# A state-space layer and a gated FFN in one kernel: decays computed early, the first pair left unnormalised, two input loads moved

## The chip, the cores and the metric

The kernel runs on one core of a Trainium2 chip. The metric is the device time of one execution in microseconds. Engines are named as the profile names them: PE (TensorE), DVE (VectorE), ACT (ScalarE), POOL (GpSimd) and SP (SyncE, which here only issues DMAs). L12 is line 12 of the kernel before.

## The reference

Inputs are x (4, 8, 768, 32), a (4, 8, 768), B and C (4, 8, 768, 16), all float32: batch, heads, sequence, and head or state size. The first half is a linear recurrence with a decay per step, written in chunks; the second half is a gated FFN over all 3072 tokens (256 to 1536 to 256).

```python
log_a = np.log(np.clip(a, 1e-06, 1.0))
for c in range(nc):                                   # chunks of 32
    cum = np.cumsum(la, axis=-1)
    L = np.exp(cum[..., :, None] - cum[..., None, :]) * causal
    M = np.einsum('bhin,bhjn->bhij', Cc, Bc) * L
    y_intra = np.einsum('bhij,bhjd->bhid', M, xc)
    y_inter = np.einsum('bhin,bhnd->bhid', Cc, state) * np.exp(cum)[..., None]
    y[:, :, sl] = y_intra + y_inter
    state = decay_full * state + sum_j Bx             # Bx: B outer x, decayed to the chunk's end
...
x = y.transpose(0, 2, 1, 3).reshape(B * S, H * D)
out = (np.maximum(x @ w_gate, 0.0) * (x @ w_val)) @ w_out
```

The kernel uses longer chunks than the reference (128 positions, in pairs of 256) and bfloat16 matmuls.

## The kernel before

**Tiling.** The 3072 tokens are 12 pairs of 256 positions, three pairs to a batch; a pair holds two chunks. The FFN runs over 6 blocks of 512 tokens, two pairs each. Before the loop over blocks, pairs 0 and 1 are done by straight code; in block b the FFN of block b runs while the recurrence of later pairs is worked in between. The order of instructions on each engine is the order of the program text: `in_order` chains them, and there is no planner.

**Decays.** A running product of a over each window of 256 positions is a scan on DVE (`product`, L215). `a_first` holds the first window of two batches (16 rows), `a_sb` all 96 windows. Each position's decay has to lie on the partition of that position, so the products are turned by float32 matmuls: `dec_wide` (L232, four matmuls) for the pairs below `NWIDE` = 4, whose positions lie two to a partition, and `dec_all` (L242, two matmuls) for all. `wfac` and `fac` hold, for B, one over the decay, and for C, the decay. The right operand normalises by the decay at the window's end: `pfirst` (the identity times one over the last product, L221 and L222) for pair 0 and the first window of batch 1, `pick` (L190, L827) for the rest.

**One pair.** `scale_bc` (L334) multiplies B and C by their factors into bf16; `transp` and `bevac`, `cevac` (L378 to L415) turn them to BT and CT; `G` (L444) multiplies them into four PSUM banks, `gevac` (L458) masks these on ACT (with POOL's causal selection) and DVE; `back` turns BT back; `astep` (L500) accumulates the state matmuls in `A_ps`; `sevac` (L517) copies the state to `Sd`; `Dm` and `inter` (L623, L599) make y, and `yevac` (L637) writes yT. Between windows of one batch the state is multiplied by `over`, the decay over a window, per partition (head). `over` is made by `dec_end` (L255), which broadcasts the last products to all partitions, and by `over_sum` and `over_sum2` (L260, L269) on DVE, which keep of each partition its own head.

**FFN.** `gvh_mm`, `gvh_relu`, `gvh_mul` (L744 to L765) do half a block (256 tokens) for one f of 12, `gv` (L731) a whole one (512); gate and val lie in the five shared PSUM banks (tag "shared"). `fout` (L775) multiplies by w_out.

**Queues.** SP issues a, and then most loads of B, C and x, in order; ACT issues three early loads; POOL issues the weights. `held` (L850) loads a pair behind a small memset on DVE, so that the issue waits until DVE reaches it. `keep_warm` (L198) issues matmuls of ones whose result is not used.

**The early order.** Pair 0: scan of `a_first`, `dw` (L819, its decays), scaling (L822, L823), transposes, G, back; then `d12` (L881, decays of pairs 1 and 2), the state step, Dm, inter, yevac; pair 1 the same way, with the first FFN matmuls in between. `dall` and the end decays are made at L930 to L935, copied by ACT at L953 to L957.

Of the kernel before, what the change touches and what calls it, by code (L numbers as in the profile page):

```python
# [8 lines left out]
FP32 = mybir.dt.float32  # L9
# [20 lines left out]
def kernel(  # L30
# [84 lines left out]
    even = const.tile([128, 24], FP32)  # L115
# [11 lines left out]
    load_bc(0, 1, nc.sync)  # L127
    new_x(0)
    load_x(0, 1, nc.scalar)
# [74 lines left out]
    keep_warm(6)  # L204
    keep_warm(1, 384)
# [3 lines left out]
    cp_first = glob.tile([2 * NH, 256], FP32)  # L209
    rfirst = const.tile([2 * NH, 1], FP32)  # L210
    pfirst = const.tile([2 * NH, 2 * NH], FP32)
# [8 lines left out]
    product(cp_first, a_first, 2 * NH)  # L220
    nc.vector.reciprocal(rfirst, cp_first[:, 255:256])  # L221
    nc.vector.tensor_scalar_mul(pfirst, identf[0:2 * NH, 0:2 * NH], rfirst)  # L222
    product(cp, a_sb, W3 * BH)
# [18 lines left out]
    def dec_all(d):  # L242
        for i in range(2):
            nc.tensor.matmul(
                out=d[:, i].rearrange("p w b h -> p (w b h)"),
                lhsT=cp[:, i * 128:(i + 1) * 128],
                rhs=pick.rearrange("p w h -> p (w h)"),
                start=(i == 0), stop=True, skip_group_check=True)


    ends = const.tile([W3 * BH, 128], FP32)
    over = const.tile([128, NB], FP32)
    over2 = const.tile([128, NB], FP32)

    def dec_end(d):  # L255

        nc.tensor.matmul(out=d, lhsT=ends, rhs=pick[:, 1], start=False, stop=True,
                         skip_group_check=True)

    def over_sum(de):  # L260
        own = smask.rearrange("p t (q d) -> p (t q) d", q=4)[:, :, 0]
        prod = const.tile([128, NB, 8], FP32)
        nc.vector.tensor_tensor(
            out=prod, in0=de.rearrange("p (b h) -> p b h", b=NB),
            in1=own.rearrange("p (o h) -> p o h", o=1).to_broadcast([128, NB, 8]),
            op=ALU.mult)
        nc.vector.tensor_reduce(out=over, in_=prod, op=ALU.add, axis=mybir.AxisListType.X)

    def over_sum2(de):  # L269
        own = smask.rearrange("p t (q d) -> p q t d", q=4)[:, :, :, 0]  # L270
# [608 lines left out]
    for i in range(2):  # L879
        load_x(2, i, nc.sync)  # L880
# [275 lines left out]
```

## Time and profile before

| | |
|---|---|
| time, median of 3 runs | 123.42 us (122.86 to 124.12) |
| the profiled execution's own time | 123.24 us |
| its span in the profile | 121.5 us, 3331 instructions |
| busy: PE, DVE, ACT, POOL | 97%, 74%, 61%, 43% |
| DMA traffic | 13.69 MB, mean 113 GB/s |

The span is the profiled part of the execution, from the first instruction to the last; the time holds 1.7 us more. A line of the timeline gives start, length, engine, line, operation, written tile, read tiles, shapes, and how many equal instructions were merged; in brackets the engine's idle time before it and what ended it. A float32 matmul shows as two passes. Matmul ends are modelled, so spacing from start to start says more than length.

### The profile page before, as it was taken

The numbers are of one execution on the slowest core, as the hardware profiler recorded it, in microseconds if no ns is written. First come the engines' busy times: TensorE is split into PE (matmuls) and PEld (weight loads), VectorE is DVE, ScalarE is ACT, GpSimd is POOL, SyncE is SP. The second block draws the span as 40 slices with busy tenths as digits, with TensorE's granted clock in tenths as the row PEclk, the third lists the DMA queues.
The fourth block names the chain that finished last, engine by engine and source line by source line (L and its number), as shares of the span: only waits on it lengthen the run. The fifth ranks groups of instructions, "written<-read, shape, count | busy, mean of one in ns | idle before, by whom it ended". The sixth has DMA issues, their size and how long they took to land.

```text
span 121.5 us, 3331 instructions
## 1 busy us (share of the span) xinstructions
PE 117.3 (97%) x1238; PEld 75.3 (62%) x1238; DVE 89.6 (74%) x214; ACT 73.8 (61%) x160; POOL 52.1 (43%) x105
## 2 busy tenths in 40 slices
PE   7999999999999999999999999999999999999990
PEld 2446854676786477888477644578544677444790
DVE  5978878986999956899876588765778766578500
ACT  4177886840898734888744767625767445776340
POOL 6879999842615073768058252633400033000000
PEclk9999999999999999999999999999999999999999
DMA  3999999959997999799996799941300002200022
GB/s 59 212 195 172 191 197 206 187 86 126 165 105 157 98 125 154 91 131 218 117 148 139 73 127 113 291 94 58 115 0 5 0 0 92 86 0 0 0 86 86
DMA packets 80591, 13.69 MB, mean 113 GB/s; under 512 B 73424, under 2 KB 80576, under 8 KB 80576
## 3 DMA queue, kind: packets, MB, share of 16 engines
q1 hardware_dynamic: 73088, 10.54, 55.4%
q0 software_dynamic: 4080, 2.36, 13.8%
q10 hardware_dynamic: 3408, 0.59, 2.6%
q8 instruction: 9, 0.15, 0.6%
q14 instruction: 6, 0.05, 0.1%
HBM read 11.12 MB, written 3.15 MB: 117 GB/s over the span
## 4 chain that ended last, share of the span: by engine, by line
PE 93%; DVE 4%; issue 0%; DVEq 0%
PE o L783 25%; PE val L738 19%; PE gate L738 19%; PE gv L753 13%; PE w L200 4%; PE g L452 2%; PE g L491 2%; PE y L678 1%; PE y L630 1%; PE o L795 1%; PE tp L389 1%; DVE gs L475 1%; DVE CT L415 1%; DVE Sm L546 1%; PE y L619 1%; DVE bs L344 1%
## 5 line engine op out<-in xcount | busy, mean ns | idle before, releaser
L742 DVE TENSOR_TENSOR h<-r,val 128x512 bf16<-128x512 bf16 x54 | 36.9, 687 | 9.3 <-ACT r L741 6.4
L741 ACT ACTIVATE r<-gate 128x512 bf16<-128x512 f32 x54 | 32.3, 597 | 12.1 <-PE gate L738 11.3
L783 PE MATMUL o<-wo,h 128*128 128x256 bf16 x276 | 33.5, 273 | 0.0
L738 PE MATMUL val<-yT,wv 128*128 128x512 bf16 x108 | 32.6, 379 | 0.0
L738 PE MATMUL gate<-yT,wg 128*128 128x512 bf16 x108 | 32.6, 379 | 0.0
L783 PEld LDWEIGHTS <-h 128*128 128x128 bf16 x276 | 25.8, 98 | 5.4 <-issue 1.2
L171 POOL TENSOR_SCALAR_AFFINE_SELECT gs<-gs 128x512 bf16<-128x512 bf16 (+1 forms) x24 | 12.2, 533 | 22.1 <-ACT gs L464 22.1
L475 DVE TENSOR_TENSOR gs<-g,masks 128x512 bf16<-128x512 f32 x24 | 15.4, 685 | 6.0 <-PE g L491 2.8
L738 PEld LDWEIGHTS <-wv 128*128 128x128 bf16 x108 | 10.4, 98 | 12.8 <-DMA wv<-in_moe_w_val_dram 0.8
L738 PEld LDWEIGHTS <-wg 128*128 128x128 bf16 x108 | 10.4, 98 | 11.1
L464 ACT CAST gs<-g 128x512 bf16<-128x512 f32 x12 | 7.0, 587 | 15.7 <-PE g L452 7.3
L763 DVE TENSOR_TENSOR h<-r,gv 128x256 bf16<-128x256 bf16 x36 | 13.9, 417 | 0.9 <-ACT r L760 0.7
L760 ACT ACTIVATE r<-gv 128x256 bf16<-128x256 f32 x36 | 13.6, 388 | 1.2
L753 PE MATMUL gv<-yT,wg 128*128 128x256 bf16 x72 | 13.9, 273 | 0.0
L753 PE MATMUL gv<-yT,wv 128*128 128x256 bf16 x72 | 13.8, 273 | 0.0
L297 POOL TENSOR_TENSOR bz<-bcr,fac 128x512 bf16<-128x512 f32 x6 | 6.4, 1060 | 11.7 <-DMA bcr<-in_B_dram 9.4
L811 ACT COPY ob<-o 128x512 f32<-128x512 f32 x11 | 6.5, 592 | 4.1 <-PE o L783 4.0
L318 ACT CAST yT<-y 128x512 bf16<-128x512 f32 (+1 forms) x9 | 4.6, 528 | 5.4 <-PE y L678 3.4
L318 POOL CAST xb<-xr 128x512 bf16<-128x512 f32 (+1 forms) x10 | 6.0, 597 | 4.2 <-DMA xr<-in_x_dram 3.1
L753 PEld LDWEIGHTS <-wv 128*128 128x128 bf16 x72 | 7.0, 98 | 0.8
L753 PEld LDWEIGHTS <-wg 128*128 128x128 bf16 x72 | 6.7, 98 | 1.1 <-issue 0.2
L200 PE MATMUL w<-const-bfloat16-1.0 128*128 128x512 bf16 (+3 forms) x16 | 6.2, 511 | 0.8 <-PEq L1140 0.8
(119 smaller groups left out, 110.5 us busy)
## 6 DMA issues: line engine op xcount, KB each, us to landing
xr<-in_x_dram SPq DMA_DIRECT2D x23, 128.0 KB, 3.3
out_dram<-ob SPq DMA_DIRECT2D x9, 256.0 KB, 2.7
bcr<-in_B_dram SPq DMA_DIRECT2D x16, 64.0 KB, 3.0
bcr<-in_C_dram SPq DMA_DIRECT2D x16, 64.0 KB, 3.0
wg<-in_moe_w_gate_dram POOLq DMA_DIRECT2D x6, 128.0 KB, 5.5
wv<-in_moe_w_val_dram POOLq DMA_DIRECT2D x6, 128.0 KB, 5.4
wo<-in_moe_w_out_dram POOLq DMA_DIRECT2D x3, 256.0 KB, 6.9
out_dram<-ob SPq DMA_DIRECT2D x4, 128.0 KB, 2.2
```

The lines of the kernel that those rows point to most:

```text
L171: nc.gpsimd.affine_select(out=dst, in_=dst, pattern=pattern, compare_op=ALU.is_ge, fill=0.0, base=0, channel_multiplier=-1)
L200: nc.tensor.matmul(out=w[:, 0:cols], lhsT=nc.const_aps.tensor(1.0, [128, 128], BF16), rhs=nc.const_aps.tensor(1.0, [128, cols], BF16), sta ...
L318: (eng.copy if eng is nc.scalar else eng.tensor_copy)(out=out, in_=in_)
L464: nc.scalar.copy(out=d[:, 0], in_=g[0])
L475: nc.vector.tensor_tensor(out=d[:, q], in0=g[q], in1=m, op=ALU.mult)
L738: nc.tensor.matmul(out=o, lhsT=w_tile(ws, f, k), rhs=yT[:, k, tk], start=(k == 0), stop=(k == 1), skip_group_check=True)
L741: nc.scalar.activation(r, g, AF.Relu)
L742: nc.vector.tensor_tensor(out=fst[b][:, f], in0=r, in1=v, op=ALU.mult)
L753: nc.tensor.matmul(out=gv_[:, j], lhsT=w_tile((wgs, wvs)[j], f, k), rhs=yT[:, k, tk], start=(k == 0 and not (early and j)), stop=(k == 1), ...
L760: nc.scalar.activation(r[:, 0:256], fst[b, f, u][:, 0], AF.Relu)
L763: nc.vector.tensor_tensor(out=fst[b][:, f, u * 256:(u + 1) * 256], in0=fst.pop((b, f, u, "r"))[:, 0:256], in1=fst.pop((b, f, u))[:, 1], op ...
L783: nc.tensor.matmul(out=o[:, ts % 2], lhsT=fst[b][:, f, ts * 128:(ts + 1) * 128], rhs=wo[:, f], start=(f == 0 and new), stop=(f == NF - 1), ...
```

## The change

It does five things.

- **Pair 0 is not normalised.** `a_first` is 8 rows instead of 16; `rfirst` and `pfirst` go, and `dw` multiplies by the identity. The state after pair 0 is therefore scaled by the window's decay when it is read: `sevac` multiplies by a fifth column of `over` and keeps a float32 copy, `before[0]`; the next state steps start anew and add `before[0]`, or `before[1]`, which is `before[0]` times `over` of batch 0, made on POOL.
- **The scan of all of a** stands behind the scaling of pair 0, `rmid` and `pick` behind CT.
- **Loads.** C of pair 0 goes second on ACT's queue, x of pair 0's second chunk to SP; its cast goes from DVE to ACT. x of pair 2 is loaded behind h of f = 8 of block 0 (before: ahead of `d12`), and so x of pair 3 stands behind it; the cast of pair 2 moves into the first third of `fout`, that of pair 3 from POOL to ACT.
- **All decays early.** `dec_wide` for pairs 1 and 2, and for pair 3, `dec_all` and a new `dec_middle` fill one PSUM tile, `decays`, in the place of `d12` and two fillers. `dec_middle` makes `over` by five one-column matmuls against `head_of`, which five ACT copies fill at the start. `dec_end`, `over_sum`, `over_sum2` go.
- **Filler.** `keep_warm` calls are shortened or dropped.

```diff
-    a_first = glob.tile([2 * NH, 256], FP32)
-    nc.sync.dma_start(out=a_first, in_=a[0:2, :, 0:256].rearrange("b h s -> (b h) s"))
+    a_first = glob.tile([NH, 256], FP32)
+    nc.sync.dma_start(out=a_first, in_=a[0, :, 0:256])
...
     load_bc(0, 0, nc.scalar)
-    load_bc(0, 1, nc.sync)
+    load_bc(0, 1, nc.scalar)
     new_x(0)
-    load_x(0, 1, nc.scalar)
+    load_x(0, 1, nc.sync)
     load_x(0, 0, nc.sync)
...
-    keep_warm(6)
-    keep_warm(1, 384)
+    keep_warm(5)
+    keep_warm(1, 256)
...
-    product(cp_first, a_first, 2 * NH)
-    nc.vector.reciprocal(rfirst, cp_first[:, 255:256])
-    nc.vector.tensor_scalar_mul(pfirst, identf[0:2 * NH, 0:2 * NH], rfirst)
-    product(cp, a_sb, W3 * BH)
+    product(cp_first, a_first, NH)
...
+    head_of = const.tile([W3 * BH, NB + 1, 128], FP32)
+    over = const.tile([128, NB + 1], FP32)
+
+    def middle_heads(eng):
+        for n in range(NB + 1):
+            heads = "p (q t o) -> p q t o" if n in (2, 3) else "p (t q o) -> p q t o"
+            b = n % NB
+            copy(eng, head_of[:, n].rearrange("p (q t n) -> p q t n", q=4, t=2),
+                 pairs[:, int(n < NB), b * NH:(b + 1) * NH].rearrange(heads, t=2, o=1).to_broadcast(
+                     [W3 * BH, 4, 2, N]))
+
+    def dec_middle(d):
+        for n in range(NB + 1):
+            nc.tensor.matmul(out=d[:, n:n + 1], lhsT=head_of[:, n], rhs=cp[:, 255:256],
+                             start=False, stop=True, skip_group_check=True)
...
-                start=(c == 0 or c == NC - 2), stop=True, tile_position=(0, 32 * q),
+                start=c in (0, 2, NC - 2), stop=True, tile_position=(0, 32 * q),
...
-            nc.scalar.copy(out=n, in_=A_ps[0][:, 0, 0:64])
+            A = A_ps[0][:, 0, 0:64]
+            if c == 1:
+                nc.scalar.copy(out=n, in_=A)
+            elif c == 2:
+                nc.scalar.mul(n, A, over[:, NB:NB + 1])
+                nc.scalar.mul(before[0], A, over[:, NB:NB + 1])
+            else:
+                nc.vector.tensor_tensor(out=n, in0=A, in1=before[0], op=ALU.add)
...
-            nc.vector.tensor_scalar_mul(n, a, over[:, b:b + 1])
+            if b:
+                nc.vector.tensor_scalar_mul(n, a, over[:, b:b + 1])
+            else:
+                nc.vector.scalar_tensor_tensor(
+                    out=n, in0=a, scalar=over[:, 0:1], in1=before[1], op0=ALU.mult, op1=ALU.add)
...
+    middle_heads(nc.scalar)
...
-    dw = bank("dw", (128, 2, 16))
-    dec_wide(dw, pfirst, cp_first)
-    nc.vector.reciprocal(wfac[:, 0, 0], dw[:, :, 0:8])
+    dw = bank("dw", (128, 2, 8))
+    dec_wide(dw, identf[0:NH, 0:NH], cp_first)
+    nc.vector.reciprocal(wfac[:, 0, 0], dw)
     scale_bc(0, nc.vector, B_)
-    scale_bc(0, nc.vector, C_, dw[:, :, 0:8])
-
-    nc.vector.tensor_copy(wfac[:, 3, 1], dw[:, :, 8:16])
-    nc.vector.reciprocal(rmid, cp[:, 255:256])
-    nc.vector.tensor_scalar_mul(pick[:, 0], pairs[:, 0], rmid)
+    scale_bc(0, nc.vector, C_, dw)
+    product(cp, a_sb, W3 * BH)
+
     keep_warm(1)
-    keep_warm(1)
-    keep_warm(1, 128)
+    keep_warm(1, 384)
...
     cevac(0, nc.scalar, nc.vector, again=tp2)
+    nc.vector.reciprocal(rmid, cp[:, 255:256])
+    nc.vector.tensor_scalar_mul(pick[:, 0], pairs[:, 0], rmid)
...
-    x_cast(0, 1, nc.vector)
+    x_cast(0, 1, nc.scalar)
...
-    new_x(2)
-    for i in range(2):
-        load_x(2, i, nc.sync)
-    d12 = mm.tile([128, 2, 2, 8], FP32, tag="tp", name="d12")
-    dec_wide(d12, pick[:, 1:3, 0:8])
-    nc.scalar.copy(out=wfac[:, 1:3, 1].rearrange("p w r h -> p r w h"), in_=d12)
-    nc.vector.reciprocal(wfac[:, 1, 0], d12[:, :, 0])
-    keep_warm(1)
-    keep_warm(1)
+    decays = mm.tile([128, 256], FP32, tag="tp", name="decays")
+    d123 = decays[:, 0:48].rearrange("p (r w h) -> p r w h", r=2, w=3)
+    middle = decays[:, 48:49 + NB]
+    dall = decays[:, 64:256].rearrange("p (i b w h) -> p i b w h", i=2, b=NB, w=W3)
+    dec_wide(d123[:, :, 0:2], pick[:, 1:3, 0:8])
+    dec_wide(d123[:, :, 2], pick[:, 0, 8:16])
+    dec_all(dall)
+    dec_middle(middle)
+    nc.scalar.copy(out=wfac[:, 1:4, 1].rearrange("p w r h -> p r w h"), in_=d123)
+    nc.vector.reciprocal(wfac[:, 1, 0], d123[:, :, 0])
     astep(0, 0)
     sevac(0, 0)
-    keep_warm(1)
-    nc.scalar.copy(out=ends, in_=cp[:, 255:256].to_broadcast([W3 * BH, 128]))
+    nc.scalar.copy(
+        out=fac.rearrange("p b (w i) j h -> p i (b w) j h", i=2)[:, :, :, 1],
+        in_=dall.rearrange("p i b w h -> p i (b w) h"))
+    nc.scalar.copy(out=over, in_=middle)
...
-    dec_all(dall)
-    dec_end(de_ps)
     astep(1, 0)
...
-    nc.scalar.copy(out=de, in_=de_ps)
-    for w in range(W3):
-        nc.scalar.copy(
-            out=fac[:, :, 2 * w:2 * w + 2, 1, :].rearrange("p b i h -> p i b h"),
-            in_=dall[:, :, w])
     new_bs(3)
     scale_bc(3, nc.gpsimd)
+    nc.gpsimd.tensor_scalar_mul(before[1], before[0], over[:, 0:1])
     zero_padded()
-    to_x(2, nc.gpsimd)
...
-                if f == 5:
-                    over_sum(de_ps)
                 if f == 7:
                     sevac(1, 1)
+                if f == 8:
+                    held(P, bc=False)
...
+                if third == 0:
+                    to_x(P, nc.gpsimd)
                 if third == 1:
                     G(P)
                     gevac(P)
-                    to_x(Q, nc.gpsimd)
...
             foevac(b, 1)
+            to_x(Q, nc.scalar)
...
-            over_sum2(de)
```

More of the change, by code (lines that the diff above doesn't have):

```diff
@@ L202, in keep_warm @@
                 rhs=nc.const_aps.tensor(1.0, [128, cols], BF16), start=True, stop=True)
-    keep_warm(6)
-    keep_warm(1, 384)
-    cp_first = glob.tile([2 * NH, 256], FP32)
-    rfirst = const.tile([2 * NH, 1], FP32)
-    pfirst = const.tile([2 * NH, 2 * NH], FP32)
+    keep_warm(5)
+    keep_warm(1, 256)
+    cp_first = glob.tile([NH, 256], FP32)
     cp = glob.tile([W3 * BH, 256], FP32)
@@ L244, in dec_all @@
             nc.tensor.matmul(
-                out=d[:, i].rearrange("p w b h -> p (w b h)"),
-                lhsT=cp[:, i * 128:(i + 1) * 128],
-                rhs=pick.rearrange("p w h -> p (w h)"),
+                out=d[:, i], lhsT=cp[:, i * 128:(i + 1) * 128],
+                rhs=pick.rearrange("p w (b h) -> p b w h", b=NB),
                 start=(i == 0), stop=True, skip_group_check=True)
-    ends = const.tile([W3 * BH, 128], FP32)
-    over = const.tile([128, NB], FP32)
-    over2 = const.tile([128, NB], FP32)
@@ L255, in dec_end @@
[L255 to L267, printed above, removed]
@@ L511, in astep @@
                 lhsT=st[p]["B"][i][:, 32 * q:32 * q + 32], rhs=xi[:, q],
-                start=(c == 0 or c == NC - 2), stop=True, tile_position=(0, 32 * q),
+                start=c in (0, 2, NC - 2), stop=True, tile_position=(0, 32 * q),
                 skip_group_check=True)
     NTILE = 2
+    before = [const.tile([128, 64], FP32, name="before%d" % k) for k in range(2)]
     def sevac(p, i):
```

18 lines of the change are left out of this document (2 added, 16 removed).

## The prediction

> **What bounds the kernel now.** I read the page first: the engine table, then the chain that ended last.
>
> ```profile
> span 121.5 us, 3331 instructions
> PE 117.3 (97%) x1238; PEld 75.3 (62%) x1238; DVE 89.6 (74%) x214; ACT 73.8 (61%) x160; POOL 52.1 (43%) x105
> ...
> PE 93%; DVE 4%; issue 0%; DVEq 0%
> ```
>
> PE is 97% busy and carries 93% of the chain. But the first 14 us are another stage: there PE's time holds filler (L200, the keep_warm matmuls), and what ends last is a relay of DVE, ACT and PE. From about 14 us to the end PE runs back to back, so a microsecond lost ahead of it comes out at the end, unless a later wait takes it up. So I read the change by what it does to that relay and to the few later waits. Next the timeline of 3 to 14 us (start, length, engine, line):
>
> ```profile
> 3.25 0.15 DVE L221 RECIPROCAL rfirst<-cp_first 16x1 f32<-16x1 f32 x1
> 3.44 0.22 DVE L222 TENSOR_SCALAR pfirst<-identf,rfirst 16x16 f32<-16x16 f32 x1
> 3.80 0.62 PE L236 MATMUL dw<-pfirst,cp_first 16*64 16x16 f32 x8
> 3.81 0.69 DVE L216 TENSOR_TENSOR_SCAN cp<-a_sb,zero 96x256 f32<-96x256 f32 x1 [0.15 <-DMA a_sb<-in_a_dram]
> 4.48 0.26 DVE L821 RECIPROCAL wfac<-dw 128x16 f32<-128x16 f32 x1
> 5.18 0.48 DVE L344 TENSOR_TENSOR bs<-bcr,dw 128x128 bf16<-128x128 f32 x2
> 6.89 0.40 PE L452 MATMUL g<-CT,BT 32*128 32x256 bf16 x8
> 7.44 0.43 PE L236 MATMUL d<-pick,cp 96*64 96x16 f32 x8
> 8.34 0.21 PE L509 MATMUL A_ps<-xb,bx 128*32 128x64 bf16 x4
> 8.62 0.41 DVE L479 TENSOR_TENSOR gs<-g,masks 128x256 bf16<-128x256 f32 x1
> 8.96 0.25 DVE L884 RECIPROCAL wfac<-d 128x16 f32<-128x16 f32 x1
> 9.13 0.83 DVE L344 TENSOR_TENSOR bs<-bcr,wfac 128x128 bf16<-128x128 f32 x3
> 10.22 0.59 DVE L415 TENSOR_SCALAR CT<-tp,tmask 128x256 bf16<-128x256 bf16 x2
> 10.87 0.40 PE L452 MATMUL g<-CT,BT 32*128 32x256 bf16 x8
> 12.29 0.73 ACT L318 CAST xb<-xr 128x256 bf16<-128x256 f32 x2
> 12.35 0.58 PE L244 MATMUL dall<-pick,cp 96*128 96x96 f32 x4
> 12.77 0.33 PE L257 MATMUL dall<-pick,ends 96*128 96x32 f32 x2
> 13.03 0.21 PE L509 MATMUL A_ps<-xb,bx 128*32 128x64 bf16 x4
> ```
>
> The reader is to see three things. Pair 0's G starts at 6.89 behind decays, scaling and transposes. Pair 1's G (10.87) hangs on DVE: mask (L479), reciprocal of the decays (8.96), scaling (9.13), CT (10.22 to 10.81). And the decays for all pairs (L244, L257) sit between 12.35 and 13.03.
>
> **The early part: a gain of 0.44 us.** The reciprocal and the product of the first decays (L221, L222) go, so the decay matmuls can follow the scan's end (3.22) and not pfirst's (3.66), with the same hand-over of 0.14: 3.36 instead of 3.80. PE is free: one 512-column filler and 128 columns fewer are 0.43 + 0.11 us, so filler that was issued until some 3.7 ends near 3.2. The scan of all of a (0.69), which ran until 4.50 ahead of the reciprocal at 4.48, goes behind the scaling. So reciprocal, scaling, transposes and G come 0.44 earlier, G at 6.45, if C has landed. It landed at 5.12 (issued 1.72, 3.4 us); now it is issued at 1.42, where x took 3.3, so 4.72, and it is wanted at 4.74. Landing as late as before would leave nothing of the 0.44; more than 0.44 there is not. I take 0.44, since the slot's own row says 4.72. The scan now ends at 5.85, ahead of the second transposes (5.90); the rest (rmid, pick) ends at 6.76, before PE wants it at 7.3. The cast of x moves to ACT, between CT (ends 6.2) and the first G copy (6.85): hidden, as are the five head_of copies, five of some 0.30 (L890's row, same tile) in ACT's empty time before 5.3.
>
> **The decays moved up: a loss of 1.16 us at the same place.** In the slot of eight matmul passes (7.44 to 7.80, 0.36) now stand 8 + 8 such passes, 4 of dec_all and 10 of dec_middle (5 float32 matmuls, two passes each as in L257's row). The 64-column passes take 0.045 each; L244's four 128-column passes take 0.42 from start to start, 0.105 each. dec_middle moves one column, but loads 128 columns of weights each time, so 10 x 0.105 = 1.05. Sum 0.36 + 0.36 + 0.42 + 1.05 = 2.19, from 7.00 to 9.19. No row has a one-column pass; bounds 0.045 and 0.13 (L257's own spacing) give 0.45 to 1.30 for dec_middle.
>
> What waits for it matters more than PE's time. In the order of the built program the copy of wfac on ACT waits for one count that PE adds at the last of these matmuls, not after its own, and the reciprocal on DVE waits for that copy. So: last result 9.34, copy 0.22, hand-overs of 0.06, reciprocal at 9.68. Before it was at 8.96, held by L479, which with the early gain would free it at 8.52. 9.68 against 8.96 is +0.72 net (-0.44 and +1.16), and from there DVE's row runs as before: scaling 9.85, yT 10.60, CT 10.94, G of pair 1 at 11.59. Behind the wait on ACT stand Sd, the fac and over copies and yT, all done before 10.9.
>
> **Taking dall out of 12.35 to 13.03: no gain.** PE has 0.68 us less to do there, but the next matmuls (13.03) need the casts of x of pair 1, which end ACT's row after G (12.29 to 13.02, now +0.72). PE will wait in the place of that work. The scaled Sd adds one ACT operation of 0.2, inside ACT's wait for G. So pair 1's outputs, and all of dense PE, come 0.72 later. The later de and fac copies, over_sum and over_sum2 (0.18 + 0.46 on ACT, 0.39 twice on DVE) leave engines that were not last there: zero; at most 0.1.
>
> **Waits behind it.** The waits view has PEld at L738 waiting for wv, 0.8 us in two, and in the timeline the second one costs PE 0.15 (18.28 to 18.43). Coming later, PE finds wv there: -0.15. Then POOL:
>
> ```profile
> 16.51 2.14 POOL L161 DMA_DIRECT2D wo<-in_moe_w_out_dram  x3
> 18.68 2.35 POOL L344 TENSOR_TENSOR bs<-bcr,wfac 128x256 bf16<-128x256 f32 x4
> 20.74 0.28 DVE L538 TENSOR_SCALAR carry<-A_ps,over 128x64 f32<-128x64 f32 x1
> ```
>
> carry (20.74) now also needs before[1], which POOL makes behind these weight issues and four scalings. POOL's row shifts by 0.66 (its masks wait for ACT's copy of G), so scaling ends at 21.69 and before[1], 0.445 by L713's row, at 22.13. DVE reaches carry at 21.35 and stands 0.8 us. Queued behind are h of f = 8 and 9; h8 then ends at 23.50 (carry and Sm 0.7, h 0.68). Five shared banks turn over, so the gate of f = 11 takes the bank of f = 8's val: PE wants it at 22.55 + 0.57 = 23.12 and gets it at 23.55. +0.43. If POOL were on time it would be 0; if the 0.8 came through whole, 0.8.
>
> **x of pairs 2 and 3.** Two 128 KB issues of SP leave 11.86 to 16 and go behind memsets after h8 and h10; B and C of pair 3 stand ahead, untouched. x of pair 2 is issued at 23.55 and 24.0. The issues that started at 23.8 took 3.6 and 4.3 us; so x lands by 28.3, the cast on POOL (0.61) ends by 28.9, wanted at 28.20 + 1.0. x of pair 3, issued behind h10 at 25.3 and 25.9, lands near 30.2; its cast, now on ACT (0.61), ends at 30.8, wanted at 30.05 + 1.0. Hidden, by 0.2 to 0.3 us: zero, and up to 0.8 if landing slips by a microsecond.
>
> **Filler and clock.** Weight loads of 128x128 bf16 are 0.15 us long up to the one at 6.15, and 0.09 at 6.86: PE speeds up in between. By the Trainium skill (TensorE: Matmul & The Clock Gate, Part 1) PE runs at half rate until one busy window of about 3.4 us of a free-running count is over, so the moment hangs on time, not on how much filler there is. By that rule the sum stays as it is, or, if the new gaps spoil a window, one more window is slow; that is the last rival.
>
> **Sum.** -0.44 + 1.16 - 0.15 + 0.43 = +1.0 on the profiled execution's own 123.24 us (span 121.5): 124.24. The median shown is 0.18 above that run, so 124.4.
>
> **The rivals.**
>
> *The decays cost half.* If one-column passes go at 0.045, the decays end 0.6 earlier and the reciprocal is held by DVE at about 8.85: -0.11, with wv -0.26. The carry then waits all the same (POOL -0.11, before[1] at 21.4, h8 ends at 22.75, bank wanted at 22.29): +0.5. Together +0.25: 123.7. For: one column; against: both 128-column rows are paced by their weights.
>
> *Faster, all of it kept.* If the copy is released by its own matmuls and x of pair 1 is there in time, -0.44 - 0.68 - 0.15 = -1.27 and no carry wait: 122.15. For: PE's filler was idle time by name; against: the single count, and ACT's row to 13.02.
>
> *Slower, x of pair 3.* x's small pieces move slowly beside weights: the pair-2 loads issued at 11.86 and 15.27 took 10.8 and 10.5 us. If wo, later by 0.66, still holds the engines at 25, x of pair 3 lands a microsecond or more past 30.2, and the state matmuls that PE then wants (L569, 30.05 before) wait: from 30.4 on each microsecond counts whole. +1.0 + 0.8: 125.2. Against: the page's GB/s falls from 187 to 86 in the slice from 24.3 us on.
>
> *Slower, the clock.* Slow until past 9.2, G and the decays run at half pace: between +1.1 (weight loads 0.15 for 0.10) and +2.2 (double): about 125.9. Against: gaps grow by only some 0.4 us.
>
> **Chances.** Forecast 0.48; half cost 0.24; faster 0.07; x late 0.14; clock 0.07. Range 122.9 to 125.6: from decays nearly free to x late. The forecast's own spread is 123.9 to 124.9. A measurement of this kernel tells about 1% (1.23 us; its three runs span 1.26) from no change, so the bounds are 122.2 and 124.65: the forecast sits below the upper one and passes it in about a third of its cases (0.16), with both slow rivals 0.37; faster 0.07; within 0.56.
>
> **What would show it.** Right: G of pair 0 near 6.45; 30 decay passes in some 2.2 us after it; L880's reciprocal near 9.7; G of pair 1 near 11.6 and PE idle before 13.6; DVE standing at the carry for POOL. Wrong: the reciprocal before 9.0, dw still near 3.8, no DVE wait for POOL, or PE waiting for x of pair 2 or 3.

## The result, and the profile after

The changed kernel takes 127.64 us (median of 6 runs, 125.75 to 129.72); the kernel before, beside it on the same chip, takes 123.36 us. The ratio is 1.0274, with a 95% interval of 1.0221 to 1.0327. The prediction was 124.4 us with a range up to 125.6. The forecast gave +1.0 us; it became +4.28.

Ratios leave out the runs that lie more than 1.5% above a kernel's fastest: three of the changed kernel's six, the profiled one among them, so that its ratio (3.4 us) lies below that of the medians (4.28 us).

The page of the profiled execution (127.78 us), the same lines as before:

```profile
span 126.1 us, 3351 instructions
...
PE 120.9 (96%) x1249; PEld 78.5 (62%) x1249; DVE 88.4 (70%) x207; ACT 76.1 (60%) x164; POOL 51.9 (41%) x105
...
PE 95%; DVE 1%; issue 1%; ACT 0%
```

PE's share of the chain rises from 93% to 95% and DVE's falls from 4% to 1%. The early relay, in which DVE ended last, has become a stretch in which PE ends last. The timeline of that stretch (start, length, engine, line; in brackets the idle time before and who ended it):

```profile
3.35 0.60 PE L231 MATMUL dw<-identf,cp_first 8*64 8x8 f32 x8
6.52 0.61 PE L433 MATMUL g<-CT,BT 32*128 32x256 bf16 x8
7.39 1.05 PE L231 MATMUL decays<-pick,cp 96*64 96x16 f32 x16
8.37 1.17 PE L239 MATMUL decays<-pick,cp 96*128 96x96 f32 x4
9.33 2.19 PE L258 MATMUL decays<-cp,head_of 96*128 96x1 f32 x10
11.55 0.20 ACT L879 COPY wfac<-decays 128x48 f32<-128x48 f32 x1 [3.26 <-PE decays L258]
11.78 0.26 DVE L880 RECIPROCAL wfac<-decays 128x16 f32<-128x16 f32 x1 [2.89 <-ACT wfac L879]
14.10 0.61 PE L433 MATMUL g<-CT,BT 32*128 32x256 bf16 x8
16.42 0.21 PE L490 MATMUL A_ps<-xb,bx 128*32 128x64 bf16 x4
```

Here dw starts 0.45 earlier than before and G of pair 0 0.37 earlier. Then 30 decay passes stand from 7.39 to 11.45, where PE turns to the state matmuls: 4.06 us instead of the forecast's 2.19. ACT stands 3.26 us for the last of them and DVE 2.89 us for ACT: the single count that the forecast had read. The reciprocal is 2.82 later than before, G of pair 1 3.23, the state matmuls of pair 1 3.39.

What doubled the price shows in the lengths of the weight loads on PE's load row. Two loads of before, then the changed kernel:

```profile
8.48 0.10 PEld L200 LDWEIGHTS <-const-bfloat16-1.0 128*128 128x128 bf16 x1
10.22 0.10 PEld L753 LDWEIGHTS <-wv 128*128 128x128 bf16 x1
```

```profile
9.18 2.25 PEld L258 LDWEIGHTS decays<-cp,head_of 96*128 96x128 f32 x10
13.53 0.15 PEld L746 LDWEIGHTS <-wv 128*128 128x128 bf16 x1
15.47 0.36 PEld L746 LDWEIGHTS <-wg 128*128 128x128 bf16 x2
17.74 0.21 PEld L746 LDWEIGHTS <-wg 128*128 128x128 bf16 x2
```

A single bf16 load of 128x128 takes 0.15 us at 13.53, and two back to back take 0.36 at 15.47; from 17.4 on, two take 0.21. Before, the single load was at 0.10 from 8.5 on. PE thus runs at about half its rate from its first matmul to about 16 us, where before it changed to the full rate at about 6.3. The page's PEclk row (the granted clock, in tenths) does not show this first slow stretch: it reads 9 in every slice before, and after in all but the last:

```profile
PEclk9999999999999999999999999999999999999998
```

A later fall of the rate is recorded, as e1 below shows. For the runs without a trace the mean granted clock tells of such falls: it was 0.986 in two of the three runs of the changed kernel that the ratio uses (125.75 and 126.74 us). If the clock was 0.50 while it was down, as in e1, that is some 3.5 us of half rate (an estimate: 0.014 of spans of 124 and 124.9 us, divided by 0.5). In the other four it was 0.997 or more, the profiled run among them. So the half rate seems to have come in two forms: in some runs PE reached the full rate late, in others it reached it and fell back. Only the first is seen in a trace of this kernel.

Later, the carry:

```profile
22.11 2.39 POOL L325 TENSOR_TENSOR bs<-bcr,wfac 128x256 bf16<-128x256 f32 x4
24.45 0.47 POOL L945 TENSOR_SCALAR before<-before,over 128x64 f32<-128x64 f32 x1
24.96 0.28 DVE L530 SCALAR_TENSOR_TENSOR carry<-A_ps,over,before 128x64 f32<-128x64 f32 x1 [0.81 <-POOL before L945]
27.57 0.27 PE L414 MATMUL bt<-ident,BT 128*128 128x128 bf16 x2 [0.63 <-DVE CT L396]
```

DVE stands 0.81 us for before[1]. PE feels it not at a bank of the FFN but at the back transpose of pair 2, which waits for CT, queued on DVE behind the carry: the shift grows there from 3.31 (gate of f = 11, 25.86 against 22.55) to 4.16 (27.57 against 23.41). Behind that, before's own pause of 0.25 us ahead of y (L619, at 29.65) is no longer there, and the shift settles at 3.73: PE's last group of output matmuls starts at 120.91 against 117.18. I call this start the end of PE's chain in what follows, since the landing of the output behind it varies by up to 0.9 us from run to run; 0.86 of the span's excess lies there. The trace of before is itself on the long side: in e6 below, where PE's early stage is that of before, neither this pause nor the 0.15 us for wv is there, and PE's chain ends at 116.67, 0.51 earlier.

### The profile page after: what moved, and what is told of

It is laid out like the page before. It is cut to its first block, busy times and chain, and to the rows that moved or that the text cites. A ratio compares the mean times of both kernels' runs of the same rounds, so it can differ in the third digit from the quotient of the medians.

```text
span 126.1 us, 3351 instructions
## 1 busy us (share of the span) xinstructions
PE 120.9 (96%) x1249; PEld 78.5 (62%) x1249; DVE 88.4 (70%) x207; ACT 76.1 (60%) x164; POOL 51.9 (41%) x105
## 3 DMA queue, kind: packets, MB, share of 16 engines
q0 software_dynamic: 4080, 2.36, 14.5%
## 4 chain that ended last, share of the span: by engine, by line
PE 95%; DVE 1%; issue 1%; ACT 0%
PE o L776 25%; PE gate L731 18%; PE val L731 18%; PE gv L746 14%; PE w L200 3%; PE g L433 2%; PE g L472 2%; PE y L623 2%; PE decays L258 2%; PE y L671 1%; PE tp L370 1%; PE o L788 1%; PE bt L414 1%; PE decays L239 1%; PE decays L231 1%
## 5 line engine op out<-in xcount | busy, mean ns | idle before, releaser
L731 PEld LDWEIGHTS <-wv 128*128 128x128 bf16 x108 | 10.6, 98 | 12.6 <-issue 0.2
L746 PE MATMUL gv<-yT,wg 128*128 128x256 bf16 x72 | 14.7, 285 | 0.0
L746 PE MATMUL gv<-yT,wv 128*128 128x256 bf16 x72 | 14.4, 281 | 0.0
L278 POOL TENSOR_TENSOR bz<-bcr,fac 128x512 bf16<-128x512 f32 x6 | 6.3, 1057 | 12.5 <-DMA bcr<-in_B_dram 5.4
L746 PEld LDWEIGHTS <-wv 128*128 128x128 bf16 x72 | 7.3, 102 | 1.0
L299 POOL CAST xb<-xr 128x512 bf16<-128x512 f32 (+1 forms) x9 | 5.3, 594 | 3.6 <-DMA xr<-in_x_dram 3.5
L299 DVE CAST yT<-y 128x256 bf16<-128x256 f32 (+1 forms) x7 | 3.7, 548 | 3.6 <-PE y L671 2.0
```

Of the source, the lines that this page charges most:

```text
L299: (eng.copy if eng is nc.scalar else eng.tensor_copy)(out=out, in_=in_)
L731: nc.tensor.matmul(out=o, lhsT=w_tile(ws, f, k), rhs=yT[:, k, tk], start=(k == 0), stop=(k == 1), skip_group_check=True)
L746: nc.tensor.matmul(out=gv_[:, j], lhsT=w_tile((wgs, wvs)[j], f, k), rhs=yT[:, k, tk], start=(k == 0 and not (early and j)), stop=(k == 1), ...
```

## The experiments

The theory after the result: the forecast's chain of waits is right, and the miss is PE's rate. Two parts of the change could lower it, the thinner filler and the decay passes. The rival: the passes or their wait simply cost more than priced, whatever the rate. Each run is compared with the kernel before, run beside it on the same chip; positions in a trace are compared with the trace of before above.

### Thinner filler alone (e2_light_before)

The kernel before, with only the changed kernel's `keep_warm` calls of the first five us:

```diff
-    keep_warm(6)
-    keep_warm(1, 384)
+    keep_warm(5)
+    keep_warm(1, 256)
...
-    keep_warm(1)
-    keep_warm(1)
-    keep_warm(1, 128)
+    keep_warm(1)
+    keep_warm(1, 384)
```

> The kernel before with only the filler of the changed kernel (five of 512 and one of 256 columns, then 512 and 384). Theory A: the clock opens late here too, weight loads stay at 0.15 us past 7, and the time rises by 1 us or more, to 124.4 to 126. Theory B: opens as before, near 6.5; 123.0 to 123.6.

Measured: 124.74 us, ratio 1.0102 (1.0008 to 1.0196); PE's chain ends 1.69 later than before. A load at half rate in its load row:

```profile
11.50 0.15 PEld L753 LDWEIGHTS <-wv 128*128 128x128 bf16 x1
```

Before, the load of the same line at 10.22 took 0.10. Two back to back take 0.36 at 13.44 and 0.21 at 14.15. So in this run 896 filler columns less are enough to keep PE at half rate for some seven us more, with the granted clock at 1.00 throughout. The pause that this opens is 0.46 us, ahead of dw. It need not happen each time: the interval of the ratio nearly reaches 1, and one of the four runs, at 123.15 us, is no slower than before.

### Full filler under the change (e1_filler)

The changed kernel with before's `keep_warm` calls in those two places:

```diff
-    keep_warm(5)
-    keep_warm(1, 256)
+    keep_warm(6)
+    keep_warm(1, 384)
...
-    keep_warm(1, 384)
+    keep_warm(1)
+    keep_warm(1, 128)
```

> The changed kernel with the filler ahead of pair 0's G put back to what the kernel before has (six of 512 columns and one of 384 ahead of the decays of pair 0, two of 512 and one of 128 behind them). Theory A, the thinner filler lets the clock open late: weight loads of 128x128 shrink from 0.15 to 0.10 us near 6.5 as in the kernel before, the 30 decay passes take some 2.2 us instead of 4.06; dw starts 0.5 later, which gives back the early gain; 123.3 + 1.0 + 0.5 = 124.8. Theory B, the decay matmuls themselves, with few columns moved, keep PE slow whatever stands ahead: the passes still take about 4, and the time is that of the changed kernel or 0.4 above it, 127 to 128.

Measured: 125.23 us, ratio 1.0182 (1.0112 to 1.0252). Half the answer: PE is fast from about 6.1 on, the 128-column passes take 0.105 to 0.128 each, and then PE falls back. Here the clock row shows it:

```profile
PEclk9995589999999999999999999999999999999999
7.13 0.11 PEld L414 LDWEIGHTS <-BT 128*128 128x128 bf16 x2 [0.21 <-issue]
8.40 1.28 PEld L258 LDWEIGHTS decays<-cp,head_of 96*128 96x128 f32 x10
11.36 0.15 PEld L746 LDWEIGHTS <-wv 128*128 128x128 bf16 x1
```

Between 7.35 and 9.70 PE issues decay passes without a pause, and behind them its loads are back at 0.15. Read in narrow stretches, the granted clock is 1.00 to 9.3, 0.50 from 9.5 to 16.1, and 1.00 again from 16.3. The passes do not bring this each time: the mean granted clock was 0.972 in two of the four runs (125.81 and 125.71 us) and 1.00 in the other two (124.75 and 124.53), so by these few runs the fall cost about 1.1 us.

### The decays alone (h2_before_decays)

The kernel before, with its own filler, and the passes of the change added in the place of d12:

```diff
-    d12 = mm.tile([128, 2, 2, 8], FP32, tag="tp", name="d12")
+    decays = mm.tile([128, 256], FP32, tag="tp", name="decays")
+    d12 = d123[:, :, 0:2]
     dec_wide(d12, pick[:, 1:3, 0:8])
+    dec_wide(d123[:, :, 2], pick[:, 0, 8:16])
+    dec_all(early)
+    dec_middle(decays[:, 48:49 + NB])
```

> The kernel before with the decays of pair 3, dec_all and dec_middle added in the place of d12, as extra work whose results are not used; its own filler, its normalised pair 0 and its late decays stay. 22 passes more, 1.83 us by the forecast's prices, with the copy behind the single count: reciprocal from 8.96 to about 10.1, later waits absorb some 0.35, so +0.8, ratio 1.006 to 1.008. Rival: the passes bring the half rate by themselves; then weight loads of 0.15 are seen behind them and the ratio is 1.015 or more.

Measured: 125.27 us, all within 0.3; ratio 1.0208 (1.0186 to 1.023). The reciprocal came at 9.81, as the prices at full rate say, and the half rate came behind it:

```profile
8.27 1.20 PEld L263 LDWEIGHTS decays<-cp,head_of 96*128 96x128 f32 x10
10.08 0.10 PEld L200 LDWEIGHTS <-const-bfloat16-1.0 128*128 128x128 bf16 x1
11.86 0.15 PEld L768 LDWEIGHTS <-wv 128*128 128x128 bf16 x1
```

The rival of this run holds: the passes bring the half rate by themselves, 2.55 us where their time was worth 0.8. The granted clock is 0.50 from 10.5 to 13.7, and its mean was 0.983 to 0.986 in all four runs.

### Columns or weights (h1_wide_decays, f1_fill_decays)

Two ways to let PE move more columns in the same stretch, both on top of the full filler. The first gives each `dec_middle` pass 96 columns instead of one, with the same weights and the same number of passes (the other 95 results are not used):

```diff
-        for n in range(NB + 1):
-            nc.tensor.matmul(out=d[:, n:n + 1], lhsT=head_of[:, n], rhs=cp[:, 255:256],
-                             start=False, stop=True, skip_group_check=True)
+        for n in range(NB, -1, -1):
+            nc.tensor.matmul(out=d[:, n:n + 96], lhsT=head_of[:, n], rhs=cp[:, 160:256],
+                             start=True, stop=True, skip_group_check=True)
```

> The changed kernel with the full filler of before (125.23 us, PE back at half rate from 9.7 on), and dec_middle moves 96 columns in each of its ten passes instead of one; weights and number of passes stay. If PE falls back because the passes move too few columns, the weight loads behind 9.7 stay at 0.10, the passes stay at 0.105 each (dec_all's passes of 96 columns take that already), and the time falls to the forecast's 124.4, ratio about 1.009. Rival: it is the weight loads, or chance; then they go to 0.15 again at about 9.7 and the ratio stays at 1.018.

Measured: 124.51 us (124.31 to 125.03), ratio 1.0157 (1.0132 to 1.0181). The passes cost the same, and the rate is kept:

```profile
8.23 1.20 PEld L258 LDWEIGHTS decays<-cp,head_of 96*128 96x128 f32 x10
11.13 0.10 PEld L746 LDWEIGHTS <-wv 128*128 128x128 bf16 x1
12.34 0.21 PEld L746 LDWEIGHTS <-wv 128*128 128x128 bf16 x2
```

The second puts a 512-column filler ahead of each of the five matmuls of `dec_middle`:

```diff
     def dec_middle(d):
         for n in range(NB + 1):
+            keep_warm(1)
```

> The changed kernel with all of the earlier filler (as in the first run) and, besides, a 512-column filler ahead of each of the five dec_middle matmuls. Theory: a stretch in which PE mostly loads weights and moves few columns counts as idle, so that PE falls back to half rate behind the decays, as the first run showed from 9.7 on. With columns moved in between it stays fast: weight loads of 128x128 at 0.10 at 10 to 16 us, pair 1's G 0.33 long and not 0.55. The decays last 1.1 longer, so the time is about that of the first run, 124.8 to 125.6. Rival, PE falls back because of how long or how hard it has worked, or at fixed times: weight loads at 0.15 again from about 9.7, and 126 or more.

Measured: 125.35 us (125.28 to 125.48), ratio 1.0195 (1.0164 to 1.0226). The single bf16 loads behind the passes are at 0.10 here too; the fillers are paid for in time of their own (the passes end at 10.15).

So in e1 the rate fell behind ten loads of 128 columns of weights with one column moved, and in h1 it did not behind the same loads with 96 columns. One pair of traces could be chance, since e1 kept the rate in two runs; the granted clock of the other runs says more. Its mean was 0.996 or more in all 15 runs of h1, f1 and h4 (below, with h1's passes), and 0.986 or less in all four of h2, in three of four of f3 and in five of six of g4, which have the one-column passes back to back. The spread agrees: 0.7 and 0.2 us for h1 and f1, 4.0 for the changed kernel. The time of h1 is not the expected 1.009, though: two of the forecast's terms were left out of that expectation. The full filler holds dw at 3.80 and so gives back the early gain, and the carry costs more than priced (below).

### The forecast's sum, with the rate kept (f3_tight_filler)

The changed kernel with 128 columns more in each of three filler groups, which fills gaps only and leaves dw at 3.37:

```diff
-    keep_warm(1, 256)
+    keep_warm(1, 384)
...
-    keep_warm(1, 384)
+    keep_warm(1)
...
-    keep_warm(1, 256)
+    keep_warm(1, 384)
```

> The changed kernel with 128 columns more in each of three filler groups ahead of pair 0's G, which only fill gaps (0.17, 0.19 and 0.15 us in the trace) and delay nothing. Theory A: the gaps alone kept PE slow past 6.5; with them filled it is fast from about 6.3, the decays take 2.2 and not 4.06, as in the first run, but G of pair 0 stands at 6.5: 124.6 to 125.2. Rival, more than the gaps is missing (the decays of pair 0 come half a microsecond earlier and themselves count as idle): PE slow as before, 127.5.

Measured: 125.02 us (124.67 to 126.16), ratio 1.0183 (1.0123 to 1.0242). In the profiled run, the fastest of the four, the rate is kept, and the steps can be read against the forecast's:

```profile
7.88 1.20 PE L258 MATMUL decays<-cp,head_of 96*128 96x1 f32 x10
9.35 0.26 DVE L880 RECIPROCAL wfac<-decays 128x16 f32<-128x16 f32 x1 [1.00 <-ACT wfac L879]
11.26 0.40 PE L433 MATMUL g<-CT,BT 32*128 32x256 bf16 x8
```

The decays stand from 6.75 to 9.01 (2.26, forecast 2.19), the reciprocal comes at 9.35 (9.68), G of pair 1 at 11.26 (11.59), and PE's chain ends 0.92 later than before (1.0). That the end agrees so well is partly luck: PE was already fast at 5 us in this run, so that G of pair 0 came at 6.20 (6.45) and the steps behind it 0.33 earlier than forecast, while the carry cost more; and against e6's trace the end is 1.43 later. But nothing in this kernel holds the rate: the other three runs had a mean granted clock of 0.972 to 0.986, and in g3_tight_before1 below, with the same filler, it was lost behind the decays again.

### The carry (e5_before1_first, g3_tight_before1, h4_wide_mended)

before[1] is made ahead of POOL's scalings of pair 2 instead of behind those of pair 3, first under the change as it is, then with the filler of f3:

```diff
     new_bs(2)
+    nc.gpsimd.tensor_scalar_mul(before[1], before[0], over[:, 0:1])
     scale_bc(2, nc.gpsimd)
...
-    nc.gpsimd.tensor_scalar_mul(before[1], before[0], over[:, 0:1])
```

> The changed kernel with before[1] made on POOL ahead of the four scalings of pairs 2 and 3 instead of behind them. If the wait of carry for it (0.81 us in the trace) holds up CT and so the turn back of pair 2 on PE, the wait goes and PE gains 0.8 to 0.9: 126.5 to 127.0. If something else holds PE there, the time stays at that of the changed kernel, 127.5.

> The changed kernel with the gap-free filler (125.02 us), and before[1] made ahead of POOL's scalings of pair 2. The forecast's term: DVE stands 0.8 us at the carry, and 0.43 of it reaches the end. Then the carry has no wait for POOL and the time is 124.6, ratio 1.015. Rival: the wait ends in work that is queued anyway, since x of pair 2 comes later; then G of pair 2 or the masks wait instead and the time stays at 125.0, ratio 1.018.

Measured: 126.73 us for the first (median 0.9 under the changed kernel; the ratio, 1.0323 with 1.0266 to 1.0379, does not resolve it), and 125.15 us for the second, ratio 1.0141 (1.0091 to 1.019) against 1.0183: not resolved either, since its runs spread from 123.44 to 128.23 and its profiled run had a granted clock of 0.50 from 9.3 to 12.5, with single loads of 0.15. In both traces the wait is gone: no wait of DVE for POOL at the carry, no pause of PE at bt.

So the same edit was made where the rate stays, on h1, together with the loads and casts of x of pairs 2 and 3 back in before's place (the edit under e6_x_moves below, reversed):

> As h1_wide_decays, and before[1] made ahead of POOL's scalings and x of pairs 2 and 3 where the kernel before has them. If the rate is kept, what is left of the forecast is -0.44 + 1.16 - 0.15 = +0.57, ratio about 1.005. Rival: the rate is not kept, or the decays cost more than that; ratio 1.012 or above.

Measured: 123.81 us (123.51 to 124.05), ratio 1.009 (1.007 to 1.0109), 0.70 under h1 in the same set of runs. h1 has one pause of PE behind the early stage, 0.63 us at bt behind CT; here there is none. The line of h1:

```profile
25.11 0.27 PE L414 MATMUL bt<-ident,BT 128*128 128x128 bf16 x2 [0.63 <-DVE CT L396]
```

As PE waits for no x of pairs 2 and 3 in h1, the 0.70 is the carry's. The 1.10 that is left is twice the expected 0.57, but it fits the forecast's other terms once the early gain is taken out, which the full filler gives back here (G of pair 0 at 6.88, before at 6.89): +1.16 - 0.15 = 1.01. The trace shows the large term directly, with PE opening about as late as in before and staying fast:

```profile
8.47 1.20 PEld L258 LDWEIGHTS decays<-cp,head_of 96*128 96x128 f32 x10
10.10 0.26 DVE L884 RECIPROCAL wfac<-decays 128x16 f32<-128x16 f32 x1 [1.08 <-ACT wfac L883]
```

The reciprocal comes 1.14 behind before's 8.96, where the forecast had 1.16 without the early gain.

### x of pairs 2 and 3 alone (e6_x_moves)

The kernel before with only the loads and casts of x moved as in the change:

```diff
-    new_x(2)
-    for i in range(2):
-        load_x(2, i, nc.sync)
...
+                if f == 8:
+                    held(P, bc=False)
...
+                if third == 0:
+                    to_x(P, nc.gpsimd)
...
-                    to_x(Q, nc.gpsimd)
...
+            to_x(Q, nc.scalar)
```

> The kernel before with only the loads and casts of x of pairs 2 and 3 moved as in the change. Theory: hidden, no wait of PE for either; 123.0 to 123.6. Rival: x of pair 3 lands late or its cast on ACT holds up other work there: 124 or more, with PE waiting for the state matmuls near 30 us.

Measured: 122.74 us, ratio 0.999 (0.9965 to 1.0014). No effect. The cover is thin, however: in f1 PE stood 0.17 us for POOL's cast of x of pair 2.

### The single count (g2_split)

The decays of pairs 1 to 3 go to the free part of dw's bank, and their copy and the reciprocal stand ahead of `dec_all` and `dec_middle`, with f3's filler:

```diff
-    dec_all(dall)
-    dec_middle(middle)
     nc.scalar.copy(out=wfac[:, 1:4, 1].rearrange("p w r h -> p r w h"), in_=d123)
     nc.vector.reciprocal(wfac[:, 1, 0], d123[:, :, 0])
+    dec_all(dall)
+    dec_middle(middle)
```

> The changed kernel with the gap-free filler (125.02 us), and the decays of pairs 1, 2 and 3 written into the free part of the bank of dw, with their copy and the reciprocal emitted ahead of dec_all and dec_middle, so that the copy waits for the count of its own 16 passes. If the single count held the reciprocal, it moves from 9.35 to about 8.4 (the masks on DVE end at 8.35), and G of pair 1 from 11.26 to some 10.85: PE has other work until 9.97, so only 0.4 of the 0.95 us arrives. Time 124.6, ratio about 1.015. Rival: the reciprocal was held by something else (the masks, or the bank); it stays at 9.2 or later and the time stays at 125.0, ratio 1.018.

Measured: 125.69 us, ratio 1.0218 (1.0178 to 1.0257): no gain. The time does not settle what the split is worth, since PE fell back here too: the granted clock was 0.50 from 11.5 to 14.5 in the profiled run, and its mean 0.986 or less in four of six. The order in the trace can be read. The copy did follow its own 16 passes, and the reciprocal came at 8.59, while `dec_middle` was still running. But the longer life of dw's bank held the back transpose of pair 0 by 0.65 us (7.25 instead of 6.54), and the transposes of pair 1 stand on PE behind the rest of the passes, the state and y anyhow (10.61). So the count decides when the reciprocal comes; PE's order decides when its result is used. With all of them early, PE's 2.2 us is what is paid.

The same split together with the edit of before[1] above and the opposite of the edit of x (g4_all_mended):

> The changed kernel with four things mended: gap-free filler, own count for the decays of pairs 1 to 3, before[1] ahead of POOL's scalings, and x of pairs 2 and 3 loaded and cast where the kernel before does it. All decays stay early and pair 0 stays unnormalised. If these four account for the loss, 125.02 comes down by 0.4, 0.4 and about 0.3 to some 123.9 or lower, ratio between 1.000 and 1.009. Rival: the 14 passes of dec_all and dec_middle in the early relay (1.5 us of PE at 0.105 each) cost by themselves, and the ratio stays near 1.012 or above.

Measured: 126.05 us, ratio 1.0267 (1.0228 to 1.0307). In its profiled run, the slowest, the decays took from 8.17 to 12.22 and single loads were at 0.15; in the other five the mean granted clock was 0.972 or 0.973. The half rate hid what it was to show. h4, with wide passes, answers the question.

### Fewer passes early (e3_decays_late, f2_all_three, g1_best, h5_best_act)

Only the 16 passes for pairs 1 to 3 and the one column that pair 0's state needs stay early; `dec_all` and the other eight passes of `dec_middle` go back to where `dall` stood before. First under the thin filler:

```diff
-    dec_all(dall)
-    dec_middle(middle)
+    dec_middle(middle, (NB,))
...
     gvh_mm(0, 2, 0)
+    dec_all(dall)
+    dec_middle(late_middle, range(NB))
     astep(1, 0)
```

> The changed kernel with dec_all and four of the five dec_middle matmuls put back to where the kernel before makes its decays for all pairs (behind the FFN matmuls of f = 1 and 2), and their two copies on ACT put back too; only 16 + 2 passes stay early. Theory B: the 18 passes take 1.0 (PE fast) to 1.5 us (PE slow), the reciprocal of pair 1's decays comes at 8.9 to 9.4 instead of 11.8, and the clock opens soon after; the time falls to 123.6 to 124.8. Theory A: the reciprocal comes at 9.4, but PE stays slow until past 12; 125 to 126.

Measured: 125.09 us, ratio 1.0157 (1.0091 to 1.0224) against the changed kernel's 1.0274. The profiled run, at 129.47 the slowest of four, had PE at half rate to about 22 us; two others had a mean granted clock of 0.986. Then with f3's filler, two fillers behind the early passes, and before[1] ahead of the scalings of pair 3:

```diff
+    keep_warm(1)
     astep(0, 0)
     sevac(0, 0)
+    keep_warm(1)
...
+    nc.gpsimd.tensor_scalar_mul(before[1], before[0], over[:, 0:1])
     new_bs(3)
     scale_bc(3, nc.gpsimd)
-    nc.gpsimd.tensor_scalar_mul(before[1], before[0], over[:, 0:1])
```

> The changed kernel with three repairs: filler without gaps ahead of pair 0's G and around its decays, only the 16 + 2 decay passes that are wanted at once left early (the rest where the kernel before has them), and before[1] made ahead of pair 3's scaling. Theory (PE's rate, decays in the way, carry waiting): PE is fast from about 6.3 on, the reciprocal comes at 8.5 to 8.9 instead of 11.8, no wait at carry; the early gain of 0.4 is left: 122.8 to 123.6. Rival, the filler still leaves PE slow: 124.5 or more.

Measured: 123.45 us over ten runs, ratio 1.0037 (1.0012 to 1.0061). The rate is kept from 6 on, and the mean granted clock was 0.995 or more in all ten; the reciprocal comes at 8.52 and G of pair 1 at 10.42, 0.45 ahead of before. That gain is spent on the eight late passes (0.81 us, where before has two passes of `dec_end`): the state matmuls of pair 1 start at 13.32, before at 13.03. It is the best version of the change that was run, and it does not beat the kernel before. The last two take these eight passes out too, with `dec_end` and `over_sum` as before, and before[1] on DVE, then on ACT one f later:

```diff
-    dec_middle(late_middle, range(NB))
+    dec_end(de_ps)
...
+                if f == 5:
+                    over_sum(de)
+                    nc.vector.tensor_scalar_mul(before[1], before[0], over[:, 0:1])
```

> Only the early part of the change is kept: pair 0 unnormalised, scan of all of a behind its scaling, decays of pairs 1, 2 and 3 and the one column of dec_middle that pair 0's state needs early, gap-free filler; dec_all, dec_end and over_sum at the place of the kernel before, before[1] on DVE behind over_sum, x of pairs 2 and 3 as changed. The version with eight late passes of dec_middle measured 123.45, with the state matmuls of pair 1 at 13.32; without these passes they come at some 12.9 (before 13.03), and the time is 0.3 to 0.5 lower: 123.0, ratio about 0.998. Rival: a later wait (y of pair 2, x of pair 2) takes it back and the ratio stays at 1.002 or above.

> As g1_best, with before[1] made on ACT behind the relu of f = 6 instead of on DVE. In g1_best the one DVE instruction for before[1] took 4.11 us and ended within 0.1 us of POOL's memsets, and PE then stood 2.69 us. If that was the loss, it is gone, the bank of f = 8 is free in time, and the time is 123.0 to 123.4, ratio 0.998 to 1.002. Rival: C of pair 0, which landed 0.8 us late there, was the loss; then the ratio stays above 1.008.

Measured: 128.52 us (124.81 to 130.15) and 127.13 us, ratio 1.0368 (1.0328 to 1.0407): both expectations missed. The first shows one instruction with a strange length:

```profile
20.02 4.11 DVE L1025 TENSOR_SCALAR before<-before,over 128x64 f32<-128x64 f32 x1
...
21.35 2.72 POOL L297 MEMSET bz<- 128x1024 bf16 x3
...
24.21 0.59 PE L758 MATMUL val<-yT,wv 128*128 128x512 bf16 x2 [2.69 <-DVE h L762]
```

On ACT the same product took 0.35 us and PE's 2.69 us wait was gone, so that part was the DVE instruction. The rival was right as well: in both, C of pair 0 landed so late that DVE stood 0.8 us for it (in the changed kernel none), and in the second PE was back at half rate (granted clock 0.50 from 8.5 to 14.5). Why C, issued at the same time, lands later there stays open, and so does the rest of their loss.

## Why the prediction was wrong

**What bounds the kernel, and the early part: right.** Predicted -0.44 for G of pair 0, measured -0.37, from dw at 3.35 (forecast 3.36).

**The decays: the mechanism right, the price of a pass wrong.** This is the step that failed: the term +1.16 took for granted that PE is at full rate when it reaches the passes. "0.105 each" and "0.045 each" were read from rows of the kernel before that stand behind 7.4, at full rate. In the changed kernel a pass with 128 columns of weights takes 0.21 to 0.24. The whole stretch, 4.06 instead of 2.19, is 1.87 of the miss, and from the reciprocal to G of pair 1 another 0.41 (2.32 us instead of 1.91). At full rate the prices hold: 1.20 us of weight loads for the ten `dec_middle` passes in f3 and h1, and in h4 the reciprocal 1.14 later, which also ends the rival "the decays cost half".

**Filler and clock: wrong in its reason.** The text let the moment of speeding up hang on time alone and gave the clock 0.07, because "gaps grow by only some 0.4 us". e2 shows that thinner filler alone can move that moment from 6.3 to about 13.9, and h2 that the passes alone bring the half rate. The Trainium skill (TensorE: Matmul & The Clock Gate, Part 1) says that PE is at half rate until a busy window of about 3.4 us, and again after an idle window of that length. The two rates agree with the loads of 0.15 and 0.10 here, and the length with the some 3.4 us for which the granted clock was at 0.50 in h2, g2 and g3; in e1 it was about twice that. "Idle" does not agree: in e1 no pause of PE over 0.21 us lies between 4.74 and 9.70, and the rate was lost all the same. And the first slow stretch of the changed kernel's profiled run lasted to about 16 us, far longer than one such window, though the profile counts PE as busy without a break from 5 us on.

The rival on the clock was the right one but too small. It had G and the decays slow until past 9.2, 125.9 us; the slow stretch of the profiled run lasted to about 16.

**Taking dall out: right.** PE's state matmuls of pair 1 at 16.42 wait for ACT's cast of x (0.21 us on the load row). **wv: right in size, not shown in its reason.** The shift falls from 3.48 at the gate of f = 4 to 3.31 at that of f = 11. But in e6, whose early stage is no later than before's (gate of f = 4 at 16.14 against 16.12), PE does not stand for wv either (gate of f = 11 at 22.40 against 22.55), so the pause can go without any shift.

**The carry: the wait right, the place and the price wrong.** 0.81 us of DVE against 0.8; but PE meets it at bt, behind CT, and pays 0.6 to 0.7 (0.63 of idle time, 0.70 between h1 and h4) instead of 0.43 at the bank of f = 11. The prediction named h of f = 8 and 9 as queued behind the carry and overlooked CT.

**x: right at zero** (e6).

Together: with the rate kept and the early gain, the change costs about 1.5 us (h1's 1.93, that is 1.57% of 122.73, less the 0.37 of the early gain); f3's profiled run, which kept both, took 1.84 more than the median of before beside it (124.67 against 122.83). The rest, about 1.9 of the ratio's 3.4 us or 2.8 of the medians' 4.28, came with the half rate. That split is worked out; no version with all the one-column passes early and back to back kept the rate in all its runs. What stays open is how PE's rate is decided in detail, and in which of its two forms the half rate struck in the changed kernel's runs that have no trace: f3 and g3 have the same filler and lost the rate in some runs and not in others.

## What to carry to other kernels

Filler, and float32 matmuls that load 128 columns of weights to move one, must be priced twice: for their own time, and for what they may do to PE's rate; read single weight loads in the stretch (0.10 or 0.15 here) before any duration of a row is carried to another place. Where small matmuls must stand in an early stage, give them more columns if they cost the same. When a wait is added to an in-order engine, go through everything queued behind it up to the next thing PE asks for, not only through the operation that looks nearest.

## What the runs showed of the hardware

- The half rate came back under continuous work: ten float32 loads of 96x128 with one column each, 1.28 us, were followed by loads of 0.15 and a granted clock of 0.50 (e1, in two of four runs; h2 in all four); with 96 columns each, in 1.20 us, by loads of 0.10 (h1, with a mean clock of 0.996 or more in all five runs).
- The granted clock showed such a fall, 0.50 for some 3.4 us (h2) or 6.8 us (e1), but not the half rate that PE starts with: in the changed kernel it read 1.00 up to 15.5 us while single loads took 0.15. There only lengths and spacing tell.
- A DVE product (128x64 float32, both operands in SBUF) took 4.11 us beside POOL's scalings and memsets and ended at 24.13, POOL's memsets at 24.07. The Trainium skill (GPSIMD Engine Reference, 1. Specifications) says that POOL's SBUF interface is shared with VectorE and that instructions of some kinds contend for it; this row agrees, but no run here took POOL's work away to show it.
